# Moving work between TensorE, VectorE and the DMA queues in the last third of a long-convolution backward pass

## The chip, the cores and the metric

The kernel runs on one core of a Trainium2 chip. The metric is the device time of one execution in microseconds, the median of several runs. The profile that is read here is of one further execution.

## What is computed

The reference is a small network of two kinds of layer, run twice each, and its gradient. Layer A is a gated long convolution; layer B is a two-matrix MLP with SiLU. All tensors are bfloat16, sequence length 2048, width 448, hidden width 1792.

```python
def A(q, k, v, shift_k, ssm_k, ssm_D):
    k_shift = causal_conv(k, shift_k)            # 4 taps per channel
    kv = k_shift * v
    y = irfft(rfft(pad(kv)) * rfft(pad(ssm_k)))[:S]   # per channel, length 2*S
    return q * (y + kv * ssm_D)

def B(x, w1, w2):
    return silu(x @ w1) @ w2

x = A_q
x = x + A(layernorm(x), ...);  x = x + B(layernorm(x), ...)
x = x + A(layernorm(x), ...);  x = x + B(layernorm(x), ...)
# outputs: x, and the gradients of A_q, A_k, A_v, A_shift_k, A_ssm_k, A_ssm_D, B_w1, B_w2
```

The convolution does not depend on x, so its spectrum is computed once, and its gradient is computed once, from the summed gradient of y.

## The kernel before

There are three parts, one after the other in the code, which overlap on the chip.

The **prefix** (`_ssm_prefix`) makes the transforms of the filter and of kv on TensorE in two stages (16 points, then 128) and stores both spectra to HBM: `spec_K` and `spec_KV`, each 128 rows (64 real parts, 64 imaginary parts) of 14 chunks of 1024 columns. The product is transformed back into `Ysb`, which is y.

The **main part** (`Main.run`) goes over four chunks of 512 rows and does both layers forward and backward in each, in a woven order that is written out by hand. It stores the activations and their gradients to HBM for the weight gradients. A job generator (`Jobs.steps`) makes the weight gradients in steps of four matmuls of 128x448 (`ps_d`, L906); every step is called by hand between other TensorE work (`jobs.run(n)`). A block of 128 hidden units is eight steps, four with the operand of the second layer pair and four with that of the first. It needs two loads of 512 KB (`dstat`, L900), which SyncE's queue issues. The other operand stays in SBUF: `go` and `X` for the gradient of w2, `n3` and `n1` for that of w1. Blocks 0 to 6 of w2 come first, then the 14 blocks of w1, then blocks 7 to 13 of w2 (L948 to L963).

The **suffix** (`_ssm_suffix`, from L1050) makes the gradients of the convolution. In order:

- Stage 1 (L1068): 16 steps of two matmuls from `Ysb`, which by now holds the gradient of y, with a job step after each. Then `n3` is loaded (L1072, L979).
- Transposes (L1092): seven groups of 16, copied to Z by ScalarE and VectorE in turn, with a job step after each. The first three Z tiles are one tile, `Zw`.
- The inverse loop (L1133): seven rounds. Each round does the second transform stage of the next two chunks (`spectrum`, L1105) and then four products (`inverse`, L1118): for each of two chunks, the conjugate product with the KV spectrum and with the K spectrum. A product is two VectorE multiplications (`pa` with Z, `pb` with `xsw`, which is Z with real and imaginary halves exchanged) and 16 matmuls that accumulate both with two constant matrices (L226, L227). Three job steps follow each product. The spectra come in by `spec_load`, once a round, into two buffers.
- The deferred layer-norm rows (`APart`, L1015): the gradient of A_q needs eight row pairs, each with three loads and 16 VectorE operations. One pair goes behind the third group of transposes, one behind each round.
- gkv (L1163): the gradient of k_shift and of v. gK (L1181): the gradient of ssm_k, four pieces; of each, VectorE copies one column into `gKD`, which is stored as the gradient of ssm_D in elements of 2 bytes.
- The shift-kernel product (L1202): 224 matmuls with 32 columns each, then a reduction on VectorE (L1208 to L1219).
- The row loop (L1221): 16 groups on VectorE, which give the gradient of A_k.
- All job steps that are left (L1230).

TensorE executes in the order of the code (`manual_schedule`). On the other engines and the queues a planner orders the instructions, and `issue_after` ties one instruction behind another; each engine and each queue then works in that order. Large tiles share slots by tag in the pool `wk`: slot WY holds Ysb, then `n3`, then `go2` (the gradient operand for the last w2 blocks); slot WT holds `w2T`, then `Zw`, then `ksf`. A tile can only be written when the earlier one in its slot has been read for the last time.

Of the kernel before, what the change touches and what calls it, by code (L numbers as in the profile page):

```python
# [17 lines left out]
P = 128  # L18
S = 2048
D = 448  # L20
# [13 lines left out]
def make_fft_consts():  # L34
# [35 lines left out]
    def inv_pair(conj):  # L70
        sa = [1.0, 1.0] if conj else [1.0, -1.0]
        sb = [-1.0, 1.0] if conj else [1.0, 1.0]
        ga = build(lambda ci, co: sa[ci] * (Ct if co == 0 else St))
        gb = build(lambda ci, co: sb[ci] * (-St if co == 0 else Ct))
        return ga, gb

    GiA, GiB = inv_pair(False)
    GiAc, GiBc = inv_pair(True)
    GiBc = np.roll(GiBc, 64, axis=0)
    Gs = np.stack([G, GiA, GiB, GiAc, GiBc], axis=1)  # L80
# [3 lines left out]
G_FWD, G_IA, G_IB, G_IAC, G_IBC = range(5)  # L84
# [36 lines left out]
def kernel(  # L121
# [34 lines left out]
    k.SPEC_d = {nm: dram.tile([128, SPEC], BF16, name=f"spec_{nm}") for nm in ("K", "KV")}  # L156
# [15 lines left out]
    k.Gsb = keep.tile([P, 5, P], BF16, name="Gsb")  # L172
# [29 lines left out]
def _fft_stage1(k, n2, rhs, A1, psum, m=None):  # L202
    nc = k.nc
    ps = psum.tile([P, 2, 512], FP32, name="ps_s1", **k.pt["s1"])
    for c in range(2):
        nc.tensor.matmul(ps[:, c, :D], lhsT=k.M1sb[:, n2 if m is None else m, c, :], rhs=rhs, start=True, stop=True)
    _copy(nc, k.bal.pick(2 * D) if m is None else nc.scalar, A1[:, :, :, n2, :].rearrange("p dh c ds -> p c dh ds"), ps[:, :, :D].rearrange("p c (dh ds) -> p c dh ds", ds=4))

# [12 lines left out]
def _fft_inv_stage2_chunk(k, pa, pb, conj, B1, ci, psum, cnd=False):  # L221
    nc = k.nc
    ga, gb = (G_IAC, G_IBC) if conj else (G_IA, G_IB)
    pv = psum.tile([P, 8, P], FP32, name="ps_v", **k.pt["v"])
    for i in range(8):
        nc.tensor.matmul(pv[:, i, :], lhsT=pa[:, i * P:(i + 1) * P], rhs=k.Gsb[:, ga, :], start=True, stop=False)  # L226
        nc.tensor.matmul(pv[:, i, :], lhsT=pb[:, i * P:(i + 1) * P], rhs=k.Gsb[:, gb, :], start=False, stop=True)  # L227
    if cnd:
        _copy(nc, k.bal.pick(1024), B1[:, :, 32 * ci:32 * ci + 32].rearrange("p q (dh ds) -> p dh q ds", ds=4),
              pv[:].rearrange("p dh (q ds) -> p dh q ds", ds=4))  # L230
    else:
        _copy(nc, k.bal.pick(1024), B1[:, 8 * ci:8 * ci + 8, :].rearrange("p a b -> p (a b)"), pv[:].rearrange("p a b -> p (a b)"))


def _swap_halves(k, dst, src):
    k.nc.vector.tensor_copy(dst[0:64], src[64:128])
    return k.nc.vector.tensor_copy(dst[64:128], src[0:64])
# [41 lines left out]
def _ssm_prefix(k):  # L279
# [4 lines left out]
    with ExitStack() as es:  # L284
# [108 lines left out]
        def cons_ka(ci, ps):  # L393
            sl = slice(ci * 1024, (ci + 1) * 1024)
            _copy(nc, bal.pick(1024), Ka[:, sl], ps[:])
            if ci % 2 == 1:
# [3 lines left out]
                nc.gpsimd.dma_start(out=k.SPEC_d["K"][:, lo:hi], in_=Ka[:, lo:hi])  # L400
# [37 lines left out]
        def cons_prod(ci, ps):  # L438
# [3 lines left out]
            if ci % 2 == 1:  # L442
                st = nc.gpsimd.dma_start(out=k.SPEC_d["KV"][:, (ci - 1) * 1024:(ci + 1) * 1024], in_=Zf[:, (ci - 1) * 1024:(ci + 1) * 1024])
# [9 lines left out]
            if len(hold) > 2:  # L453
                pa, pb, cj = hold.pop(0)
                _fft_inv_stage2_chunk(k, pa, pb, False, B1, cj, psum)

        _fft_stage2(k, Zkv, psum, cons_prod)
        for pa, pb, cj in hold:
            _fft_inv_stage2_chunk(k, pa, pb, False, B1, cj, psum)
# [379 lines left out]
class Jobs:  # L839
# [78 lines left out]
    def group(self, fts, keys, movs, fin, tags=None):  # L918
        ps = {}
        tags = tags or [None] * len(fts)  # L920
        for i, ft in enumerate(fts):
            st = self.load(keys[0], ft)
            ps[ft] = self.bank(tags[i])
# [41 lines left out]
    def go2(self):  # L965
        k = self.k
        if not hasattr(self, "go2t"):
            self.go2t = k.wk.tile([P, NT, D], BF16, name="go2", tag="WY")
# [10 lines left out]
    def load_n3(self):  # L979
        k = self.k  # L980
        self.n3 = k.wk.tile([P, NT, D], BF16, name="n3m", tag="WY")
        k.nc.sync.dma_start(out=self.n3[:], in_=_pm(k.N_d[3][:]))
# [32 lines left out]
class APart:  # L1015
# [6 lines left out]
    def fetch(self):  # L1022
# [3 lines left out]
        for nm, src, bufs in (("g", k.G1_d, 2), ("n", k.N_d[0], 1), ("y", k.Y_d, 1)):  # L1026
# [234 lines left out]
```

## Time and profile before

| What | us |
|---|---|
| runs: median (lowest to highest) | 773.59 (770.3 to 775.28) |
| profiled execution | 769.31 |
| its span | 767.5 |
| stage 1 | 526 to 546 |
| transposes | 547 to 558 |
| inverse loop, gkv follows | 563 to 674 |
| gkv, gK | 674 to 709 |
| rest | 709 to 767 |

How to read the profile: PE is TensorE, PEld its weight loads, DVE is VectorE, ACT is ScalarE, POOL is GpSimd, SP is SyncE. A row names the code line, the operation and the tiles; in square brackets stands how long the engine had been idle before it and what it waited for. "issue" is idle time for which the profile shows no cause. Waits are listed as total, number, longest. The landing time of a DMA counts from its issue.

### The profile page before, as it was taken

Reading aid. Unit: us, or ns where it says so; the run is one execution under the profiler, and the core shown is the slowest. Engines: PE = TensorE matmul, PEld = TensorE weight load, DVE = VectorE, ACT = ScalarE, POOL = GpSimd, SP = SyncE. Lnnn points to the kernel's source line nnn. Section 1 sums busy time; section 2 is a strip of 40 time slices with the busy share of each in tenths; the row PEclk is TensorE's granted clock in tenths of the full one; section 3 lists DMA queues with packets and bytes.
Section 4 is the critical chain, followed back from the end, with each engine's and each line's share of the span. In section 5 each row is a group of like instructions: output and inputs, shape, how many; then the busy total and the mean of one; then the engine's idle time right before and its main releaser. Section 6 shows DMA issues by size and latency. Waiting matters only on the chain.

```text
span 767.5 us, 12748 instructions
## 1 busy us (share of the span) xinstructions
PE 707.8 (92%) x4991; PEld 398.6 (52%) x5020; DVE 476.4 (62%) x1137; ACT 459.2 (60%) x581; POOL 127.0 (17%) x213
## 2 busy tenths in 40 slices
PE   6998779999999999999999999999979999999594
PEld 4976534445444455444445445444646666656352
DVE  4789832857685758855487526444357767760497
ACT  5878767787957878587786772214645454454000
POOL 1144210210020100201001000001212322143211
PEclk9999989999999999999999999999989999999797
DMA  9959769479968996678975993498977897689861
GB/s 319 267 168 292 282 231 233 114 190 226 218 150 187 272 223 169 131 194 210 216 190 115 218 308 131 104 246 251 397 290 243 315 326 243 203 341 364 80 207 60
DMA packets 188653, 171.28 MB, mean 223 GB/s; under 512 B 135954, under 2 KB 166802, under 8 KB 187440
## 3 DMA queue, kind: packets, MB, share of 16 engines
q1 hardware_dynamic: 173984, 113.95, 56.9%
q0 software_dynamic: 14144, 56.50, 22.1%
q8 instruction: 39, 0.64, 0.3%
q14 instruction: 22, 0.18, 0.1%
q10 hardware_dynamic: 464, 0.00, 0.0%
HBM read 73.52 MB, written 60.10 MB: 174 GB/s over the span
## 4 chain that ended last, share of the span: by engine, by line
PE 62%; ACT 12%; DVE 9%; DMA 8%; issue 7%; POOL 2%; SPq 0%; POOLq 0%; ACTq 0%; DVEq 0%
PE ps_d L906 12%; PE ps_h L603 10%; PE ps_n L671 10%; PE ps_g L644 9%; PE ps_o L625 6%; ACT dT L618 3%; DMA n3m<-N_d 2%; PE ps_d L941 2%; DMA M1sb<-c_m 2%; PE ps_v L227 2%; PE ps_v L226 2%; PE ps_t L517 2%; ACT aT L606 1%; DVE ln_st L259 1%; ACT dT L111 1%
## 5 line engine op out<-in xcount | busy, mean ns | idle before, releaser
L906 PEld LDWEIGHTS <-dstat 128*128 128x128 bf16 x800 | 77.0, 99 | 72.4 <-issue 10.4
L603 PE MATMUL ps_h<-nT,w1sb 112*128 112x512 bf16 x448 | 104.4, 379 | 5.5 <-ACT dT L111 2.5
L644 PE MATMUL ps_g<-nT,w2T 128*128 128x512 bf16 x432 | 100.4, 381 | 1.3 <-ACT nT L518 0.2
L671 PE MATMUL ps_n<-w1T,ghT 128*128 128x448 bf16 x448 | 95.3, 353 | 1.8 <-DVE ghT L656 1.7
L625 PE MATMUL ps_o<-w2sb,aT 128*128 128x448 bf16 x448 | 88.8, 352 | 0.0
L654 ACT CAST ghT<-ps_g 128x1024 bf16<-128x1024 f32 (+1 forms) x68 | 54.5, 824 | 49.7 <-PE ps_g L644 49.7
L606 ACT ACTIVATE aT<-ps_h 128x1024 bf16<-128x1024 f32 (+1 forms) x72 | 58.4, 834 | 31.6 <-PE ps_h L603 30.8
L603 PEld LDWEIGHTS <-w1sb 112*128 112x128 bf16 x448 | 43.8, 98 | 58.3 <-issue 8.7
L644 PEld LDWEIGHTS <-w2T 128*128 128x128 bf16 x448 | 43.7, 99 | 50.9 <-issue 1.8
L831 DVE SCALAR_TENSOR_TENSOR lb_v<-lb_u,n 128x448 bf16<-128x448 bf16 x48 | 29.9, 624 | 64.1 <-ACT lb_u L675 63.6
L671 PEld LDWEIGHTS <-ghT 128*128 128x128 bf16 x448 | 43.2, 98 | 44.3 <-DVE ghT L656 4.0
L625 PEld LDWEIGHTS <-aT 128*128 128x128 bf16 x448 | 43.4, 98 | 39.8
L906 PE MATMUL ps_d<-n3m,dstat 128*128 128x448 bf16 x224 | 50.1, 362 | 5.4 <-DMA n3m<-N_d 5.0
L618 ACT ACTIVATE dT<-dT 128x1024 bf16<-128x1024 bf16 (+1 forms) x64 | 54.6, 936 | 0.1
L266 POOL TENSOR_TENSOR rstd<-ln_ve,mhalf 128x2 f32<-128x2 f32 (+2 forms) x27 | 22.6, 836 | 182.4 <-DVE ln_ve L264 182.4
L111 ACT CAST dT<-ps_h 128x1024 bf16<-128x1024 f32 (+1 forms) x59 | 52.1, 901 | 0.0
L906 PE MATMUL ps_d<-n1m,dstat 128*128 128x448 bf16 x224 | 47.8, 352 | 0.1
L226 PE MATMUL ps_v<-Gsb,pa 128*128 128x128 bf16 x336 | 42.9, 219 | 3.1 <-DVE pa L449 3.0
L227 PE MATMUL ps_v<-Gsb,pb 128*128 128x128 bf16 x336 | 42.2, 219 | 2.2 <-DVE pb L450 1.9
L518 ACT COPY nT<-ps_t 128x1024 bf16<-128x1024 bf16 (+1 forms) x28 | 28.3, 1012 | 20.8 <-PE ps_t L517 20.1
L675 ACT ACTIVATE lb_u<-ps_n,rstd 128x448 bf16<-128x448 f32 x32 | 20.7, 646 | 32.2 <-PE ps_n L671 18.1
L906 PE MATMUL ps_d<-X,dstat 128*128 128x448 bf16 x176 | 38.9, 363 | 0.0
(202 smaller groups left out, 1191.7 us busy)
## 6 DMA issues: line engine op xcount, KB each, us to landing
dstat<-g_d SPq DMA_DIRECT2D x28, 512.0 KB, 5.0
dstat<-a_d SPq DMA_DIRECT2D x26, 512.0 KB, 5.6
a_d<-turned SPq DMA_DIRECT2D x16, 512.0 KB, 3.8
g_d<-turned SPq DMA_DIRECT2D x16, 512.0 KB, 3.4
a_d<-turned SPq DMA_DIRECT2D x16, 384.0 KB, 3.1
g_d<-turned SPq DMA_DIRECT2D x16, 384.0 KB, 2.7
N_d<-n POOLq DMA_DIRECT2D x10, 448.0 KB, 5.0
spec_K<-Z POOLq DMA_DIRECT2D x7, 512.0 KB, 7.2
```

What stands on the lines that cost most here:

```text
L111: nc.scalar.copy(out, in_)
L226: nc.tensor.matmul(pv[:, i, :], lhsT=pa[:, i * P:(i + 1) * P], rhs=k.Gsb[:, ga, :], start=True, stop=False)
L227: nc.tensor.matmul(pv[:, i, :], lhsT=pb[:, i * P:(i + 1) * P], rhs=k.Gsb[:, gb, :], start=False, stop=True)
L603: nc.tensor.matmul(ps[:, u, :], lhsT=self.w1sb[:, dc, ft * P:(ft + 1) * P], rhs=nT[:DC, dc, :], start=(dc == 0), stop=(dc == ND - 1))
L606: self.last_silu = nc.scalar.activation(aT[hh][:, o:o + hi - lo, :], ps[:, lo:hi, :], ACT.Silu)
L618: self.nc.scalar.activation(d[:, o:o + n, :], d[:, o:o + n, :], ACT.Derivative_silu)
L625: nc.tensor.matmul(po[:, :D], lhsT=aT[ft // 7][:, ft % 7, tl * P:(tl + 1) * P], rhs=self.w2sb[:, ft, :], start=(ft == 0), stop=(ft == NF - 1))
L644: nc.tensor.matmul(ps[:, u, :], lhsT=self.w2T[:, b, ft * P:(ft + 1) * P], rhs=gT[:, b, :], start=(b == 0), stop=(b == ND - 1))
L654: nc.scalar.copy(g, ps[:, lo:hi, :])
L671: nc.tensor.matmul(pn[:, :D], lhsT=gh[ft // 7][:, ft % 7, tl * P:(tl + 1) * P], rhs=self.w1T[:, ft, :], start=(ft == 0), stop=(ft == NF - 1))
L831: nc.vector.scalar_tensor_tensor(out=v[:], in0=u0, scalar=-1.0 / D, in1=n_t, op0=ALU.mult, op1=ALU.mult, accum_out=cp[:, 1:2])
L906: self.nc.tensor.matmul(ps[:, :D], lhsT=st[:, t, :], rhs=mov[:, t, :], start=(first and t == 0), stop=(last and t == NT - 1))
```

## The change

**Inverse.** The spectrum store becomes one tensor of 128 rows x 14 chunks x (K, KV) x 1024. `spec_load` is called for each chunk in place of each pair: it makes two transfers to 128 partitions, the 64 real rows written to both halves, and the 64 imaginary rows written to both halves. The two buffers keep their size, so each holds one chunk. VectorE forms the whole complex product: `q = Z * real`, `q2 = xsw * imaginary`, `q = q + q2`; the exchange of halves now also negates one half. TensorE does eight matmuls a product, with one constant matrix. There are four buffers for q and q2 together, where pa and pb had five. The copies out of PSUM are given to ScalarE by name.

**Operands.** `n3` and `go2` move to slot WT, `Zw` and `ksf` to slot WY. `n3` is loaded when block 5 of w2 begins, in the queue behind that block's first load.

**Rows.** `APart` is set up before stage 1; row pairs are also run behind steps 6 and 11 of stage 1, and `q_g` has three buffers.

**Tail.** The gKD copies go from VectorE to ScalarE. Three job steps follow each of the four parts of the shift-kernel product. Its reduction and its two stores move into the row loop, behind group 11.

```diff
-    k.SPEC_d = {nm: dram.tile([128, SPEC], BF16, name=f"spec_{nm}") for nm in ("K", "KV")}
+    k.SPEC_d = dram.tile([128, NCI, 2, 1024], BF16, name="spec")
...
+    GiQ = build(lambda ci, co: (Ct, -St)[ci] if co == 0 else (St, Ct)[ci])
...
 def _swap_halves(k, dst, src):
     k.nc.vector.tensor_copy(dst[0:64], src[64:128])
-    return k.nc.vector.tensor_copy(dst[64:128], src[0:64])
+    return k.nc.vector.tensor_scalar(out=dst[64:128], in0=src[0:64], scalar1=-1.0, scalar2=None, op0=ALU.mult)
...
         for i, ft in enumerate(fts):
             st = self.load(keys[0], ft)
+            if fts == (5, 6) and i == 0:
+                self.load_n3()
...
-            self.go2t = k.wk.tile([P, NT, D], BF16, name="go2", tag="WY")
+            self.go2t = k.wk.tile([P, NT, D], BF16, name="go2", tag="WT")
...
-        self.n3 = k.wk.tile([P, NT, D], BF16, name="n3m", tag="WY")
-        k.nc.sync.dma_start(out=self.n3[:], in_=_pm(k.N_d[3][:]))
+        self.n3 = k.wk.tile([P, NT, D], BF16, name="n3m", tag="WT")
+        with k.tc.issue_after(self.last_ld.ins):
+            k.nc.sync.dma_start(out=self.n3[:], in_=_pm(k.N_d[3][:]))
...
-        for nm, src, bufs in (("g", k.G1_d, 2), ("n", k.N_d[0], 1), ("y", k.Y_d, 1)):
+        for nm, src, bufs in (("g", k.G1_d, 3), ("n", k.N_d[0], 1), ("y", k.Y_d, 1)):
...
+        ap = APart(k, e1.enter_context(tc.tile_pool(name="qp", bufs=1, reuse_waits="tile")))
         for n2 in range(16):
             k.M1sb = k.m1h[n2 // 8]
-            _fft_stage1(k, n2, gY[:, n2, :], A1, psum, n2 % 8)
+            mm1 = _fft_stage1(k, n2, gY[:, n2, :], A1, psum, n2 % 8)
             jobs.run(1)
-        jobs.load_n3()
+            if n2 in (6, 11):
+                ap.run(1, mm1)
...
-            def spec_load(cp):
-                lo, hi = cp * 2048, (cp + 1) * 2048
-                nc.gpsimd.dma_start(out=kk[:, 0, :], in_=k.SPEC_d["K"][:, lo:hi])
-                nc.gpsimd.dma_start(out=kk[:, 1, :], in_=k.SPEC_d["KV"][:, lo:hi])
+            def spec_load(ci):
+                for c in range(2):
+                    src = k.SPEC_d[64 * c:64 * c + 64, ci].rearrange("(o p) m n -> o p (m n)", o=1).to_broadcast([2, 64, 2048])
+                    nc.gpsimd.dma_start(out=kk[:, c].rearrange("p m n -> p (m n)"), in_=src)
...
-                    for spec_t, B1, cnd in ((t[1], B1k, True), (t[0], B1v_, False)):
-                        pa = p1.tile([P, 1024], BF16, name="pa", tag="pab", bufs=5)
-                        pb = p1.tile([P, 1024], BF16, name="pb", tag="pab", bufs=5)
-                        nc.vector.tensor_tensor(out=pa[:], in0=Zf[cp][:, o], in1=spec_t[:, o], op=ALU.mult)
-                        last = nc.vector.tensor_tensor(out=pb[:], in0=t[2][:, o], in1=spec_t[:, o], op=ALU.mult)
-                        bal.add("dve", 2.2)
-                        _fft_inv_stage2_chunk(k, pa, pb, True, B1, ci, psum, cnd=cnd)
+                    for m in (1, 0):
+                        q = p1.tile([P, 1024], BF16, name="q", tag="pab", bufs=4)
+                        q2 = p1.tile([P, 1024], BF16, name="q2", tag="pab", bufs=4)
+                        nc.vector.tensor_tensor(out=q[:], in0=Zf[cp][:, o], in1=kks[ci][:, 0, m, :], op=ALU.mult)
+                        nc.vector.tensor_tensor(out=q2[:], in0=xsw[:, o], in1=kks[ci][:, 1, m, :], op=ALU.mult)
+                        last = nc.vector.tensor_tensor(out=q[:], in0=q[:], in1=q2[:], op=ALU.add)
+                        pv = psum.tile([P, 8, P], FP32, name="ps_v", **mm)
+                        for i in range(8):
+                            nc.tensor.matmul(pv[:, i, :], lhsT=q[:, i * P:(i + 1) * P], rhs=k.Gsb[:, G_IQ, :], start=True, stop=True)
...
                         jobs.run(3)
+                    if ci + 2 < NCI:
+                        kks.append(spec_load(ci + 2))
...
-            nc.vector.tensor_copy(gKD[:, dc:dc + 1], gK[:, 0:1])
+            nc.scalar.copy(gKD[:, dc:dc + 1], gK[:, 0:1])
...
                     nc.tensor.matmul(pd[32 * b:32 * b + 32, 0, P * r0:P * r0 + P], lhsT=gks[:, sl_, ch], rhs=kx[:, sl_:sl_ + 4, ch], start=(sl_ == 0), stop=(sl_ == 15))
-        junk = p2.tile([P, 4, 4, 32], FP32, name="skjunk", tag="gka")
-        jobs.run(4)
+            jobs.run(3)
...
+            if g != 11:
+                continue
+            junk = s_[:].rearrange("p a d -> p (a d)")[:, 0:512].rearrange("p (r u c) -> p r u c", u=4, c=32)
...
```

## The prediction

> **What bounds the kernel now.** I read the busy totals first, then TensorE's waits in the last third of the span (only code there changes much), then the busy time by stage, then VectorE in order of time, then the landing times of the spectra.
>
> ```profile
> PE 707.8 (92%) x4991; PEld 398.6 (52%) x5020; DVE 476.4 (62%) x1137; ACT 459.2 (60%) x581; POOL 127.0 (17%) x213
> ```
>
> TensorE is the bound on average; the question is which of its work and waits from 526 us on go away. Its waits between 520 and 770 us:
>
> ```profile
> PE ps_sk L1207 <- issue: 7.7, 1, 7.7
> PE ps_d L906 <- DMA n3m<-N_d: 5.0, 1, 5.0
> PE ps_gkv L1169 <- ACT gkv L1171: 1.8, 1, 1.8
> PE ps_sk L1207 <- DVE gKD L1193: 0.7, 1, 0.7
> ```
>
> Four single waits, 15.2 us. The stages (columns: stretch, length, busy us of PE, PEld, DVE, ACT, POOL, granted clock, DMA share, GB/s):
>
> ```profile
> 546.00:563.00 17.00, 11.92 (x142) 8.95 (x140) 9.47 (x20) 7.38 (x7) 2.71 (x5) 0.96 1.01 417
> 563.00:575.00 12.00, 11.61 (x65) 6.00 (x66) 6.49 (x10) 5.36 (x6) 0.54 (x1) 0.77 0.66 242
> 591.36:606.84 15.48, 15.43 (x132) 9.96 (x132) 10.98 (x28) 7.92 (x11) 5.23 (x9) 1.00 0.78 259
> 606.84:622.31 15.47, 15.42 (x132) 9.96 (x132) 10.97 (x27) 7.91 (x11) 3.58 (x7) 1.00 0.97 370
> 709.00:720.00 11.00, 3.42 (x212) 3.27 (x212) 0.05 (x1) 1.70 (x3) 2.55 (x4) 0.79 1.06 101
> 740.00:767.00 27.00, 17.41 (x93) 8.81 (x90) 23.35 (x27) 1.60 (x3) 4.88 (x9) 0.86 0.23 80
> ```
>
> The reader is to see that one round of the inverse loop (15.48 us, seven rounds) is all TensorE, with VectorE at 10.98; that both long waits lower the granted clock after them; and that at the end VectorE, not TensorE, is the busy one. Why, in VectorE's timeline:
>
> ```profile
> 708.89 0.16 DVE L1193 COPY gKD<-gK 112x1 bf16<-112x1 bf16 x1 [8.24 <-ACT gK L111]
> 721.05 0.75 DVE L1212 TENSOR_TENSOR skjunk<-ps_sk,skmask 128x384 f32<-128x384 f32 x2 [12.00 <-PE ps_sk L1207]
> 763.07 0.63 DVE L1226 TENSOR_TENSOR B1v<-gka 128x448 bf16<-128x448 f32 x1
> ```
>
> From 691 to 721 it stands behind four tiny copies and the shift-kernel product, then runs the row loop (L1223 to L1226, 2.66 us a row) to 763.7. TensorE's last result is copied at 757.49 and issued at 758.33; VectorE's last store is issued at 763.99.
>
> **Part by part**, against the profiled execution: 769.31 us, span 767.5. It lies 4.28 under the median of the runs, 773.59, so the final sum is scaled by 773.59/769.31.
>
> *n3 into the slot of w2T.* Before, its load issues at 546.23, when stage 1 has read Ysb, and lands 16.9 us later. The new slot was last read near 514, and SP issues the load behind that of block 5 at 529.10. Even 16.9 us later it is there at 546; it is needed at 558. Gone: 5.0 us, and the slow clock behind it: rounds of 2.30, 2.34 and 1.54 us (563.17 to 569.35) where a warm one takes 1.19, so 2.6. Together -7.6. Queued behind n3 on SP are three a loads and g loads (512 KB each); the first is needed at 540.4, and 2.9 MB at 319 GB/s take 9.1 us from 529.1, so it fits by 2 us. Zw, which changes places with n3, must now wait for stage 1's last read at 546.2; its first copy is at 548.30, so that costs nothing, and ksf and go2 follow the same tiles as before. What is late next: the first product's chain, a copy of 1.01, two swaps of 1.39, a product and a sum of 0.69 each, against some 2.4 us of TensorE work: +1.5 (0 to 3).
>
> *Deferred-norm rows earlier.* Two of eight row pairs move into stage 1, where VectorE is idle for 18.5 us before its copy at 548.30; each is 4.73 us of work. Their q loads land in 6.7 to 8.5 us there and have one buffer for n and y, so the second pair waits for the first, and the pair behind group 2 for the second. VectorE runs in order: if the second pair sits ahead of the Z copies, TensorE's transposes wait. Bounds 0 and 8 (one q landing, 8.5); I take +2.5, nearer zero because the 18.5 idle us hold both pairs' 9.5. On POOL the first pair's three loads (1.6 us of issue) go ahead of Minvs, not needed before 674, and of kk, needed at 560. In return rounds 6 and 7 carry no rows. The third buffer of q_g takes away POOL's six waits for the out store (29.1 us together), which lie on no path.
>
> *Single product.* A product's 16 matmuls take 0.89 us here, between job blocks:
>
> ```profile
> 571.30 0.22 PE L226 MATMUL ps_v<-Gsb,pa 128*128 128x128 bf16 x1
> 572.19 2.43 PE L906 MATMUL ps_d<-n1m,dstat 128*128 128x448 bf16 x12
> ```
>
> Eight of the 16 go: 28 x 0.445 = -12.45, and a round becomes 15.48 - 1.78 = 13.7. ACT's copies stay (all 28 are on ACT now). VectorE gains four sums a round at 0.606 spacing (2.42), and each sum needs the product before it, 0.115 later than a free one (0.45): 13.85. The swap's second half becomes a multiply by -1; no row shows that one. Its bounds are the copy (0.69 for 64x2048) and twice that, since the tensor_scalar of 128x448 (L834, 0.395) costs as much as a tensor_tensor of the same shape (0.391). I take the copy's end for the likeliest, since both run one input from SBUF, and keep 0.54 a round for the range: 13.85 to 14.4 with rows, 9.1 to 9.7 without. So VectorE passes TensorE by 0.15 to 0.7 in the five rounds with rows: 0.8 to 3.5.
>
> [...]
>
> *Spectra.* Bytes double: 28 loads of 512 KB for 14, on the same two buffers, each for one chunk, not two. POOL issues two more a round (0.54 each, it is busy under 5.3 of 15.5). A buffer's cycle is landing, 0.54 for the second issue, and four products with sums, 3.9 us; it must fit 13.7, so a load may take 9.3 us. The present ones:
>
> ```profile
> DMA to landing us min/median/max: 3.6/7.6/11.0
> DMA to landing us min/median/max: 3.9/6.6/18.0
> ```
>
> The medians (kk_c, then kk_d) fit; the loads beside ksf (9.9 and 11.0, at 370 GB/s) miss by up to 1.7; the 18.0 fell in the stretch at 417 GB/s. A round now moves 1.8 MB of dstat, 2.1 of spectra, 0.9 of rows, 0.2 of results, 5.05 MB: 369 GB/s at 13.7 us. The trace has held 417 for 17 us, so it can be moved, with little to spare. For VectorE and the buffers together I give back +4 of the 12.45 (0 to 12.45).
>
> [...]
>
> *gkv.* The 1.8 wait is for gks, whose load POOL issues at 676.28 behind the last rows' store (it waited 6.80 for it). The rows end two rounds sooner: -1.75 (0 at worst).
>
> *Shift-kernel product.* 212 small matmuls run in 3.42 us, then 7.7 us "issue". The DMA view from 709 to 713 has two instruction transfers and from 713 to 720 none; there queue 0 holds the engines for 113.6% with only 64 packets, while the gKD store (0.9 KB) needs 16.1 us and the gK store 15.0. I read it as TensorE running out of instructions while stores block the queues. After the change 12 job steps lie between its four blocks, so a block's 64 pairs and 12 job pairs, 152 instructions, go in 3.3 us: 46 per us in place of 124. The store itself stays. Gone: 7.7, 0.74, and the slow clock after it (20 matmuls from 720.94 in 6.04 us where 3.79 is warm: 2.25), -10.7; I leave +1.5 (0 to 10.7).
>
> *End.* gKD goes to ACT (four copies of about 0.2, hidden in its idle time) and the reduction (2.1 us, and two POOL issues of 0.81 and 0.55, which now go ahead of the last two row stores and delay none that is ready) behind row 11, so VectorE's 16 x 2.66 + 2.1 = 44.7 us begin when gkv ends; TensorE has 69.8 - 10.7 = 59 from there. VectorE is hidden by 14 us, and waits 2 for the product. TensorE's results end: the last issue is 5.66 earlier, its landing 4.0 where 2.2: -3.9. Were that cover gone, the end would be VectorE's again, 3.9 later.
>
> *Prefix.* Spectra stores in runs of 2 KB, not 4: VectorE already waits 2.7 for one (L557): +0.5 (0 to 3).
>
> **Sum**: -7.6 +1.5 +2.5 -12.45 +4 -1.75 -10.7 +1.5 -3.9 +0.5 = -26.4; 742.9 on the profiled scale, x 773.59/769.31 = 747.0.
>
> **Rivals.**
> 1. The loop gains nothing: VectorE with 13.85 to 14.4 and the buffers hold it at 15.48. For it: three resources within 5%. Against: TensorE needs a product only every 2.7 us and two lie ready. 742.9 + 8.45 = 751.4, 755.5 scaled.
> 2. The pause in the shift-kernel product survives, since the store that I blame stays: 742.9 + 9.2 = 752.1, 756.3 scaled.
> 3. Slower: the spectra's landing sets the round. At landing L it is L + 4.44. It eats the whole gain at 13.7 + 0.57 + 26.4/7 = 18.0, so from L = 13.6. For it: 13.7 and 18.0 are in the trace, at DMA saturation, and demand is 369 GB/s. Against: two of fourteen loads. At L = 16 a round is 20.4, 7 x 6.7 - 4 = 43 us more: 786, 790 scaled.
> 4. Nothing is given back: 732.9, 737 scaled.
>
> **How the numbers follow.** Forecast 0.45, rival 1 0.2, rival 2 0.15, rival 4 0.1, rival 3 0.1. The range runs from rival 4's 737 to 765, which takes in rivals 1 and 2, each alone and both together (764.8); outside lie rival 3 and a part of rival 4. Within 1% (about what a measurement of this kernel can tell from no change) means 765.9 to 781.3: only a mild form of rival 3 or all give-backs together. Faster 0.86, same 0.06, slower 0.08.
>
> **What would show it.** No wait of ps_d for n3m, and clock 1.00 at 563; 224 matmuls fewer, rounds of 13.7 to 14.5 us; waits of ps_v for the sums or of VectorE for kk in their place if rival 1 or 3 holds; no pause inside ps_sk; last in the chain a dout store. It would be wrong if TensorE waits at ps_tr for Z copies behind rows, or if kk lands later than 10 us throughout.

## The result, and the profile after

The changed kernel takes 890.49 us (median of 4 runs, 889.39 to 891.3), the kernel before 774.34 us on the same chip (4 runs, 770.3 to 775.28): a ratio of 1.1503, 95% interval 1.1459 to 1.1548. Forecast were 747.0 us, in a range of 737 to 765. It is 143.5 us slower than forecast, and on the other side of the kernel before.

The profiled execution after has a span of 889.0 us and a mean granted clock of 0.917 (767.5 us and 0.979 before). Start with what TensorE waited for, over the whole span. Columns: waiting instruction <- what ended the wait: us in total, times, longest.

```profile
PE ps_v L1125 <- DVE q L1122: 89.1, 9, 14.9
PE ps_tr L1091 <- DVE Zw L1095: 23.8, 1, 23.8
PE ps_d L896 <- issue: 6.9, 2, 6.5
PE ps_tr L1091 <- DVE Zg L1095: 5.7, 1, 5.7
```

The wait for n3 is gone, as forecast. In its place stand 89 us in the products, for VectorE's sums, and 30 us in the transposes, for VectorE's copies of Z. VectorE is not full there; it waits too, for loads:

```profile
DVE q_y L1035 <- DMA q_y<-Y_d: 96.2, 7, 27.4
DVE q L1120 <- DMA kk_c<-spec: 41.6, 3, 14.8
```

So look at the loads. From the page: two of its DMA counts (packets and MB), and two lines of its list of DMA issues, with the median us from issue to landing last:

```profile
DMA packets 215755, 178.65 MB, mean 201 GB/s; under 512 B 161266, under 2 KB 192114, under 8 KB 214544
...
q0 software_dynamic: 41248, 63.91, 24.3%
...
kk_c<-spec POOLq DMA_DIRECT2D x14, 512.0 KB, 19.7
kk_d<-spec POOLq DMA_DIRECT2D x14, 512.0 KB, 19.0
```

The loads have the size of those before (512 KB), and land in 19 to 20 us instead of 7.6 and 6.6. The rows' loads, whose shape the change leaves alone, are late with them: the median landing of q_y is 19.1 us, before it was 4.7. Yet the engines are not full. The stretches of the loop, with engine busy time, TensorE's granted clock (PEclk), the share of the 16 DMA engines that is busy, and GB/s:

```profile
600.00:640.00 40.00, 25.70 (x156) 13.73 (x155) 22.89 (x45) 13.40 (x15) 9.12 (x14) 0.81 0.55 146
640.00:680.00 40.00, 25.14 (x161) 14.14 (x160) 14.98 (x33) 12.26 (x16) 6.96 (x10) 0.79 0.74 180
680.00:720.00 40.00, 17.30 (x91) 9.36 (x90) 15.96 (x38) 7.10 (x9) 9.14 (x13) 0.66 0.62 169
```

146 to 180 GB/s, where the loop before moved 261 on the mean (563 to 674), and a DMA share of 0.55 to 0.74: the loads are slow although the engines have time left. The packet counts point at a reason. Before, queue 0 sent 14144 packets for 56.50 MB; now it sends 41248 for 63.91. Packets under 512 B are 25312 more (161266 - 135954), some 900 for each of the 28 spectra loads. In the trace they have 4 bytes: queue 0 has 28098 packets of that size, 2786 before. What brings them is shown below (x2).

The early row work stands in VectorE's timeline (start, duration, operation, and in brackets the idle time before it and what ended it):

```profile
543.25 0.69 DVE L1035 SCALAR_TENSOR_TENSOR q_y<-q_g,rstd,q_y 128x448 bf16<-128x448 bf16 x1 [12.39 <-DMA q_y<-Y_d]
...
575.86 0.69 DVE L1035 SCALAR_TENSOR_TENSOR q_y<-q_g,rstd,q_y 128x448 bf16<-128x448 bf16 x1 [27.41 <-DMA q_y<-Y_d]
...
580.99 1.22 DVE L1095 COPY Zw<-ps_tr 128x2048 bf16<-128x2048 bf16 x1
```

The second pair's q_y load is issued at 548.46, between the first two spectra loads (535.73 and 551.78), and lands only at 575.86. VectorE makes its first copy of Z behind that pair: at 580.99 instead of 548.30.

In the tail the four blocks of the shift-kernel product now run without a gap, but the pause follows right behind them (TensorE's timeline):

```profile
845.54 1.07 PE L1208 MATMUL ps_sk<-kx_s,gks 128*32 128x128 bf16 x32
846.54 0.55 PE L896 MATMUL ps_d<-X,dstat 128*128 128x448 bf16 x2
847.44 0.35 PE L896 MATMUL ps_d<-X,dstat 128*128 128x448 bf16 x1 [0.35 <-issue]
854.33 4.26 PE L896 MATMUL ps_d<-X,dstat 128*128 128x448 bf16 x13 [6.54 <-issue]
```

And one line settles a doubt of the forecast, the swap's second half: 0.69 us, the rate of a copy.

```profile
604.74 0.69 DVE L227 TENSOR_SCALAR xsw_c<-Zw 64x2048 bf16<-64x2048 bf16 x1
```

### The profile page after: what moved, and what is told of

It reads as the page before. It is cut to its first block, busy times and chain, and to the rows that moved or that the text cites. A ratio compares the mean times of both kernels' runs of the same rounds, so it can differ in the third digit from the quotient of the medians.

```text
span 889.0 us, 12374 instructions
## 1 busy us (share of the span) xinstructions
PE 718.9 (81%) x4796; PEld 394.3 (44%) x4796; DVE 494.2 (56%) x1161; ACT 459.6 (52%) x585; POOL 145.4 (16%) x227
## 2 busy tenths in 40 slices
DMA packets 215755, 178.65 MB, mean 201 GB/s; under 512 B 161266, under 2 KB 192114, under 8 KB 214544
## 3 DMA queue, kind: packets, MB, share of 16 engines
q0 software_dynamic: 41248, 63.91, 24.3%
## 4 chain that ended last, share of the span: by engine, by line
PE 42%; DMA 22%; issue 12%; DVE 11%; ACT 9%; POOL 3%; POOLq 0%; SPq 0%; DVEq 0%; ACTq 0%
DMA kk_c<-spec 9%; PE ps_h L593 9%; PE ps_n L661 8%; PE ps_g L634 8%; PE ps_o L615 6%; DMA q_y<-Y_d 4%; DMA out_dram<-q_g 3%; PE ps_d L896 3%; ACT dT L608 2%; DMA kk_d<-spec 2%; PE ps_d L933 2%; PE ps_t L507 1%; ACT aT L596 1%; DMA turned<-ghT 1%; DMA q_n<-N_d 1%
## 5 line engine op out<-in xcount | busy, mean ns | idle before, releaser
L896 PEld LDWEIGHTS <-dstat 128*128 128x128 bf16 x800 | 80.8, 104 | 87.5 <-issue 26.3
L634 PE MATMUL ps_g<-nT,w2T 128*128 128x512 bf16 x448 | 103.1, 384 | 0.7 <-ACT nT L508 0.7
L1125 PE MATMUL ps_v<-Gsb,q 128*128 128x128 bf16 x224 | 20.4, 244 | 89.1 <-DVE q L1122 89.1
L1035 DVE SCALAR_TENSOR_TENSOR q_y<-q_g,rstd,q_y 128x448 bf16<-128x448 bf16 x16 | 10.3, 683 | 96.2 <-DMA q_y<-Y_d 96.2
L1125 PEld LDWEIGHTS <-q 128*128 128x128 bf16 x224 | 16.7, 110 | 97.0 <-DVE q L1122 93.2
L896 PE MATMUL ps_d<-n1m,dstat 128*128 128x448 bf16 x224 | 54.6, 389 | 0.0
L896 PE MATMUL ps_d<-n3m,dstat 128*128 128x448 bf16 x224 | 54.1, 384 | 0.0
L1127 ACT CAST A1g<-ps_v 128x1024 bf16<-128x1024 f32 x14 | 14.2, 1012 | 70.3 <-PE ps_v L1125 70.3
L896 PE MATMUL ps_d<-X,dstat 128*128 128x448 bf16 x176 | 40.7, 372 | 6.9 <-issue 6.9
## 6 DMA issues: line engine op xcount, KB each, us to landing
kk_c<-spec POOLq DMA_DIRECT2D x14, 512.0 KB, 19.7
```

The lines of the kernel that those rows point to most:

```text
L634: nc.tensor.matmul(ps[:, u, :], lhsT=self.w2T[:, b, ft * P:(ft + 1) * P], rhs=gT[:, b, :], start=(b == 0), stop=(b == ND - 1))
L896: self.nc.tensor.matmul(ps[:, :D], lhsT=st[:, t, :], rhs=mov[:, t, :], start=(first and t == 0), stop=(last and t == NT - 1))
L1125: nc.tensor.matmul(pv[:, i, :], lhsT=q[:, i * P:(i + 1) * P], rhs=k.Gsb[:, G_IQ, :], start=True, stop=True)
```

## The experiments

The theory, a supposition that nothing above shows: `to_broadcast([2, 64, 2048])` makes a source whose outermost dimension is 2, and such a load runs on only 2 of the 16 DMA engines (F). Rivals: the doubled bytes (B), and the order, by which the early rows hold VectorE whatever the loads do (O).

**x1_two_halves**: the same bytes, as loads of 64 plain rows.

```diff
-  src = k.SPEC_d[64*c:64*c+64, ci].rearrange(...).to_broadcast([2, 64, 2048])
-  nc.gpsimd.dma_start(out=kk[:, c]..., in_=src)
+  for o in range(2):
+      nc.gpsimd.dma_start(out=kk[64*o:64*o+64, c], in_=k.SPEC_d[64*c:64*c+64, ci])
```

> The changed kernel with each transfer to 128 partitions cut into two transfers to 64 (same bytes, same rows read twice, 56 issues in place of 28). Theory F (few engines: a source that repeats 64 rows is carried by 2 of the 16 DMA engines, and all that POOL issues later waits behind it): the spectra land in 4 to 10 us in place of 15 to 24, and the time falls to the prediction's 740 to 765. Rival B (bytes: twice the spectra are too much for the DMA engines beside the other loads): landings stay over 13 us, the time over 860. Rival O (order: the early rows block VectorE whatever the loads do): landings fall, but the wait of ps_tr for Z copies stays near 24 us, 775 to 800.

Measured: 790.4 us (788.55 to 793.88), ratio to the kernel before 1.0226 (1.019 to 1.0262). 100.1 of the 116 us are gone, with twice the number of loads and the same bytes. Packets of queue 0, the landings of kk_c and kk_d, and TensorE's waits in the transposes:

```profile
q0 software_dynamic: 16608, 63.81, 26.3%
DMA to landing us min/median/max: 3.6/7.8/16.3
DMA to landing us min/median/max: 7.4/9.3/12.8
PE ps_tr L1091 <- DVE Zw L1095: 6.5, 1, 6.5
PE ps_tr L1091 <- DVE Zg L1095: 4.0, 1, 4.0
```

The time misses F's 740 to 765 and lies in O's range, but O's sign is not there: the waits of ps_tr for Z copies fall from 29.5 to 10.5 us. The landings are F's in the median. Packets under 512 B are 136627, 673 more than before for 42 more loads: about 16 for each additional load.

**x2_before_twice64**: the other way round, the kernel before with its 14 loads made of 64 rows sent twice (the second half of the rows is not loaded).

```diff
-  nc.gpsimd.dma_start(out=kk[:, 0, :], in_=k.SPEC_d["K"][:, lo:hi])        # and KV
+  nc.gpsimd.dma_start(out=kk[:, i, :], in_=k.SPEC_d[nm][0:64, lo:hi].rearrange("(o p) n -> o p n", o=1).to_broadcast([2, 64, 2048]))
```

> The kernel before, with the source of each of its 14 spectra loads replaced by 64 rows repeated twice (the second half of the rows is left out of the computation; count, bytes and destinations as before). Theory F: landings of 13 to 24 us and some 900 four-byte packets per load more; the time rises, by less than in the changed kernel since a buffer has a whole round: 790 to 850. Rival B: bytes are as before, so landings stay at 4 to 11 us and the time within 1% of before.

Measured: 838.78 us, ratio 1.087 (1.08 to 1.0939), median landings of 21.8 (kk_c) and 18.5 us (kk_d) at the bytes and the number of loads of the kernel before. The page:

```profile
q0 software_dynamic: 26688, 56.55, 21.4%
```

26688 - 14144 = 12544, which is 896 for each of the 14 loads, and for 0.05 MB more (56.55, before 56.50) some 4 bytes each. 896 is 14 x 64: what F would give if each of 14 engines without data had one packet for each of the 64 rows. The count of the changed kernel comes out in the same way: 28 x 896, and 16 for each of the 14 additional loads (as in x1), are its 25312. The trace does not name a packet's engine, so that two engines carry the rows is read into these counts, not shown. B is out as the main cause.

**x3_shapes**: the same in the kernel before, with the outermost dimension 16, 16, 16, 8, 4, 2 and 2 in the seven rounds (one execution, 814.66 us; the rows that are not loaded are left out).

> The kernel before with a different repeat for the loads of each round: 16 times 8 rows (first three rounds' loads), 8 times 16, 4 times 32, 2 times 64 (the last two); the other rows are left out of the computation, bytes are the same. Theory F, with as many engines as there are repeats: landings of about 4 to 8 us at 16 repeats, 5 to 9 at 8, 8 to 12 at 4, 13 to 20 at 2. Rival B: no order by repeats. A third way: any repeated source is slow alike, 13 to 20 us in all.

Landings, first and second load of a round, us: 16 (third round) 5.3 and 7.0; 8: 11.3 and 10.0; 4: 23.0 and 26.2; 2: 18.8 and 19.3, 18.2 and 19.7. (The second round's, also 16, took 17.3 and 24.4; they are issued at 541 to 544, into the stretch in which the kernel before had its 18.0.) With 16 a load is as quick as a plain one (medians of 7.6 and 6.6 in the kernel before), with 8 slower, with 4 and 2 about three times as slow. For 8 and 4 that is more than F's 5 to 9 and 8 to 12. The loads with 4 can't be compared with the others: POOL issues them right behind the load of ksf (1792 KB, 617.04, 12.4 us to landing), and how much of their 23.0 and 26.2 us is theirs stays open. The count fits F: if n repeats use n engines and each of the other 16 - n gets 128/n small packets, the loads with 8, 4 and 2 give 2 x 8 x 16 + 2 x 12 x 32 + 4 x 14 x 64 = 4608, and the page has 18752 - 14144 = 4608. So the counts agree with F in sum for repeats of 16, 8, 4 and 2; no run here has another, and the number of engines itself stays a reading. That rows are read more than once is not the cause: x1 reads its rows twice too (medians of 7.8 and 9.3 us to landing), and 16 repeats of 8 rows landed in 5.3 and 7.0.

**x4_no_early_rows**: x1 without the two row pairs in stage 1.

```diff
-            if n2 in (6, 11):
-                ap.run(1, mm1)
```

> As x1_two_halves, but the two row pairs behind steps 6 and 11 of stage 1 go back to the rounds of the loop. Theory F: within 10 us of x1, no wait of ps_tr for Z copies over 3 us; if the early rows cost as I had put it (+2.5), x4 is faster by some 2 us or slower by what two more rounds with rows cost (0.5 to 3). Rival O: faster than x1 by 15 us or more.

Measured: 781.9 us, ratio 1.0096 (1.0061 to 1.0132); 8.5 less than x1, and no wait of ps_tr for Z copies is left. The early rows cost more than the forecast's 2.5, but O's 15 were not reached.

With plain loads, x4 still stood 35 us over the forecast. The next runs take the forecast's terms one by one.

**y1_slot**: the kernel before with the new place of n3's load alone.

```diff
-  self.go2t = ..., tag="WY");  self.n3 = ..., tag="WY");  Zw = ..., tag="WT");  ksf = ..., tag="WT")
+  self.go2t = ..., tag="WT");  self.n3 = ..., tag="WT");  Zw = ..., tag="WY");  ksf = ..., tag="WY")
-  jobs.load_n3()                                  # behind stage 1
+  if fts == (5, 6) and i == 0: self.load_n3()     # in group, behind block 5's load
```

> The kernel before with the changed place of n3's load alone: Zw and ksf in buffer WY, go2 and n3 in WT, n3's load issued in the group of blocks 5 and 6; loop, row work and tail are those of before. Theory that the forecast's other terms hold and only the loads failed: the wait of 7.6 us for n3 is gone and nothing takes its place, 765 to 768 us against 774. Rival: the wait is given back, for the following waits are set by VectorE and by landings and not by PE's order: 772 to 776 us. If slower than 777, the longer life of WT or WY makes another load late.

Measured: 770.58 us, ratio 0.998 (0.9942 to 1.0019). Of the expected 7.6 us at most 4.5 are there, perhaps none: it lies between theory and rival. Its trace is of an execution of 1375.83 us and is not used here.

**y2_tail**: the new tail alone.

```diff
-  nc.vector.tensor_copy(gKD[:, dc:dc + 1], gK[:, 0:1])
+  nc.scalar.copy(gKD[:, dc:dc + 1], gK[:, 0:1])
+      jobs.run(3)            # behind each of the four ps_sk blocks
-  junk = ...; jobs.run(4)    # the reduction, ahead of the row loop
+  if g == 11: junk = ...     # the reduction, inside the row loop
```

> The kernel before with the changed tail alone: the column copies of gKD on ScalarE, three steps of the planner behind each ps_sk block, and the reduction of ps_sk behind step 11 of VectorE's row loop. Theory that the forecast's terms hold: pause 10.7 less 1.5 left, end 3.9, gkv 1.75, together about 15 us: 758 to 762 us. Rival (the pause survives and only moves behind the blocks): 5.6 us at most, 767 to 772 us, with a ps_d or ps_sk matmul that waits over 5 us for nothing that the profile shows. Third: the row loop on VectorE or its stores end the kernel: 771 or more.

Measured: 763.96 us, ratio 0.9893 (0.9862 to 0.9924): -8.3 us, between the theory's 758 to 762 and the rival's 767 to 772. TensorE's wait in the product:

```profile
PE ps_sk L1207 <- issue: 10.3, 4, 5.2
```

The pause survives (7.7 before), as the rival had it. The gain is then the shorter end and what the steps between the blocks cover; the two were not taken apart.

**y3_row_store**: the kernel before, with gKD stored in rows.

```diff
-  nc.gpsimd.dma_start(out=k.outs[6].rearrange("(c p) -> p c", p=DC), in_=gKD[:])     # 448 elements of 2 bytes
+  nc.tensor.transpose(pt[:ND, 0, :DC], gKD[:], k.ident[:DC, :DC])
+  nc.scalar.copy(gDr[:], pt[:ND, 0, :DC])
+  nc.gpsimd.dma_start(out=k.outs[6].rearrange("(c p) -> c p", p=DC), in_=gDr[:])      # 4 rows of 224 bytes
```

> The kernel before with one edit: gKD (112 partitions x 4) is transposed on TensorE to 4 partitions x 112 and stored in 4 rows of 224 bytes, where before 448 elements of 2 bytes went out one by one. Theory: it is the store of single elements that stalls the DMA engines and starves PE of instructions, so the wait inside ps_sk (8.9 us, ended by issue) falls under 2 us and the time to 764 to 768 us. Rival: the wait comes with PE's instruction transfers or with the other stores at that place: it stays over 6 us, and the time within 3 us of 774.

Measured: 767.26 us, ratio 0.9938 (0.9909 to 0.9967): -4.8 us. The wait inside ps_sk of this run:

```profile
PE ps_sk L1210 <- issue: 2.8, 1, 2.8
```

And the stretch around it, first of this run, then of the kernel before (there with TensorE's busy time alone, then granted clock, DMA share, GB/s):

```profile
700.00:720.00 20.00, 15.00 (x331) 11.24 (x329) 0.31 (x2) 5.53 (x8) 6.37 (x11) 0.99 0.77 276
```

```profile
700.00:720.00 20.00, 11.74 (x293) 0.88 1.04 217
```

The small store was the main cause: its landing falls from 16.1 to 5.1 us, the pause from 7.7 (not the expectation's 8.9) to 2.8, and the DMA share from 1.04 to 0.77 while more is moved (276 GB/s, not 217). The expected 2 us were missed by 0.8. In the trace's packet records from 700 to 760 no packet of 4096 B on queue 0 takes over 0.9 us; with the 2-byte store in place some take 7.9 (before) and 6.0 (y2). The rows of y3 go out at 716, in the middle of the product (713.3 to 720.1), so it is not that the store has merely moved out of the way.

**y4_half_loads**: x4 with the loads of the second half left out and the second multiply reading the first half's tile.

```diff
-  for c in range(2):
+  for c in range(1):
-  nc.vector.tensor_tensor(out=q2[:], in0=xsw[:, o], in1=kks[ci][:, 1, m, :], op=ALU.mult)
+  nc.vector.tensor_tensor(out=q2[:], in0=xsw[:, o], in1=kks[ci][:, 0, m, :], op=ALU.mult)
```

> The run of x4 (changed kernel, each spectra load cut in two of 64 partitions, no early rows: 781.9 us) with the loads of the spectra's second half left out: the second multiply of each product reads the first half's tile, so g_k and g_v are not computed as in the reference; every instruction of VectorE, PE and ScalarE stays. Theory that what is left over (35 us over the forecast) is the doubled bytes of the loads: 745 to 755 us, and the waits of ps_v for VectorE fall from 25 us to under 8. Rival: it is VectorE's own chain (multiply, multiply, add ahead of each product): 777 to 784 us, with the waits of ps_v as they are. In between, both have a share.

Measured: 769.11 us, ratio 0.9959 (0.9924 to 0.9995): 12.8 less than x4 (10.6 by the ratios, see below); neither theory's number. The waits of ps_v for VectorE fall from 25.1 to 12.2 us. The edit halves the number of loads along with the bytes, and the two were not told apart.

**z2_no_sums**: y4 with the 28 sums left out.

```diff
-  last = nc.vector.tensor_tensor(out=q[:], in0=q[:], in1=q2[:], op=ALU.add)
```

> The run of y4 (changed kernel, half the spectra loads, no early rows: 769.1 us) with the 28 sums of the products left out: PE multiplies the first product's tile, so the spectral products are not the reference's; both multiplies and all matmuls stay. Theory that VectorE's longer chain (three operations ahead of each product, about 17 us of sums in all) takes back the matmuls that were saved: 750 to 758 us, ps_v's waits for VectorE under 4 us (12.2 in y4). Rival: the loop goes by landings and ScalarE's copies: 765 to 770 us.

Measured: 765.43 us, ratio 0.9903 (0.9866 to 0.9941). Only 3.7 less, as the rival had it: behind loads that come late, VectorE's sums do not eat the gain. (The sums were not left out where loads land in time, as in w1 below.) In their place VectorE waits 19.0 us for kk, 7.3 in y4:

```profile
DVE q L1118 <- DMA kk_c<-spec: 9.9, 5, 4.1
DVE q L1118 <- DMA kk_d<-spec: 9.1, 3, 6.4
```

A load is asked for when two chunks earlier is done, half a round ahead; the kernel before asks a whole round ahead.

**z3_slot_tail**: the kernel before with the edits of y1 and y2, loop as before.

> The kernel before with the new place of n3's load and the new tail, the loop as before: what the changed kernel is without its single product and its early rows. If y1 and y2 add: 760 to 763 us, no wait of PE for n3, about 10 us of waits for issue left in and behind ps_sk. Then the single product at half loads (y4, 769.1) costs 6 to 9 us instead of the 8.45 that the forecast took off. Rival: the slot is worth the forecast's 7.6 once the tail doesn't wait: 755 to 758 us.

Measured: 760.72 us, ratio 0.9873 (0.9806 to 0.9941). Slot and tail add up, as expected. No wait for n3; the pause stands behind the product (8.3 us, a ps_d matmul, ended by issue).

**z1_all**: the edits of y1, y2 and y3 together.

> The kernel before with the new place of n3's load (y1: -2 us), the new tail (y2: -9 us) and gKD stored in 4 rows (y3: -6 us), and with the loop's two products, its loads and its row work as before. If the three add, less what y2 and y3 take of the same pause (the wait for issue is 7.7 us before, 2.8 with the rows): 755 to 760 us against 773. Rival: the tail's gain is the pause alone, which both take: 761 to 765 us.

Measured: 753.31 us (750.22 to 756.95), ratio 0.9772 (0.9732 to 0.9813), under the expected 755 to 760. It is the quickest version found, 137 us under the change as made, and no wait of TensorE for issue is left in it at that place.

**w1_loads_of_before**: x4 with the spectra loaded as before, whole rounds ahead, and so with half the bytes of the change.

```diff
-  def spec_load(ci):   # four loads of 64 rows a chunk, issued two chunks ahead
+  def spec_load(cp):
+      for u in range(2):
+          nc.gpsimd.dma_start(out=kk[:, u], in_=k.SPEC_d[:, 2 * cp + u])
...
+  in1=kks[cp][:, u, m, :]          # in both multiplies
```

> The run of x4 (changed kernel without early rows) with the spectra loaded as in the kernel before: two plain loads of 128 partitions a round (512 KB each), a whole round ahead; both multiplies of a product read the same tile, so g_k and g_v are not computed as in the reference, but every instruction of VectorE, PE and ScalarE is that of the changed kernel's loop. It is the forecast's own condition (loads as before) with its early rows taken away. Theory that only the loads failed the forecast's loop: 747 to 754 us, the waits of ps_v for VectorE under 4 us in all (12.2 in y4, whose loads of the same bytes are issued half a round ahead), and the stretch from the last ps_tr to the first ps_gkv 96 to 100 us (116.3 before, 112.0 in y4). Rival: VectorE's sums take the gain back whatever the loads do: 758 to 766 us, ps_v's waits 8 us or more, the stretch 105 or more.

Measured: 760.96 us, ratio 0.9838 (0.9799 to 0.9877). Half of each: the loop is right as the theory had it (99.8 us, waits of ps_v 3.1), the time as the rival. TensorE's waits, and the end of the loop in the timeline:

```profile
PE ps_gkv L1166 <- ACT gkv L1168: 11.4, 1, 11.4
PE ps_sk L1204 <- issue: 8.5, 1, 8.5
PE ps_v L1121 <- DVE q L1118: 3.1, 3, 1.3
```

```profile
656.90 0.92 PE L1166 MATMUL ps_gkv<-B1v,Minvs 128*128 128x448 bf16 x4
...
660.93 0.39 DVE L826 TENSOR_TENSOR q_g<-lb_v,q_g 128x448 bf16<-128x448 bf16 x1
...
661.62 0.55 POOL L1040 DMA_DIRECT2D out_dram<-q_g  x1 [7.74 <-DMA dstat<-a_d]
...
664.49 1.07 POOL L1145 DMA_DIRECT2D gks<-in_A_v_dram  x2 [0.44 <-issue]
...
674.39 1.70 DVE L1171 TENSOR_TENSOR gks<-gkv,gks 128x896 bf16<-128x896 bf16 x3 [10.69 <-DMA gks<-in_A_v_dram]
```

TensorE is at gkv at 656.90, but the last row pair ends on VectorE at 661.3. Its store holds POOL's queue for 7.74 us (the releaser named, a load of SP's, is not the one: the store's source is written at 660.93). Behind the store stand the tail's loads; gks lands at 674.4. So 9 us of loop became 9.6 us more of wait.

**v1_early_rows** (w1 with the change's early rows: the forecast's condition, but for the doubled bytes) and **v2_pair_at_2** (w1 with two pairs behind the third round) ask whether that last pair is the cause.

```diff
+            if n2 in (6, 11):                                   # v1
+                ap.run(1, mm1)
-                ap.run(1, inverse(cp, prev))                    # v2
+                ap.run(2 if cp == 2 else 1, inverse(cp, prev))
```

> The run w1 (changed kernel, plain loads of half the bytes, both multiplies of a product reading the same tile, so g_k and g_v are not the reference's; 761.0 us) with the change's two early row pairs put back: the forecast's condition whole, 747.0 us by its sum. Theory that the last row pair in the last round holds the tail's loads: rounds 6 and 7 then carry no rows, the wait of ps_gkv (11.4 us) falls under 4, and what the early pairs cost at the transposes (8.5 us between x1 and x4, less here, for the queues are emptier) is 2 to 5 us: 752 to 757 us. Rival (the tail's loads are bound by their bytes, whoever issues them): ps_gkv still waits 8 us or more, and the early rows' cost comes on top: 762 to 767 us.

> The run w1 (761.0 us, both multiplies of a product reading the same tile) with two row pairs behind the third round instead of one, so that the last round carries none and no pair runs ahead of the transposes. Theory that the last row pair holds the tail's loads: the wait of ps_gkv falls from 11.4 us to under 5, and 753 to 757 us. Rival (bytes of the tail, or VectorE, which is busy 18 of 20 us in the third round, passes the loss on): ps_v's waits grow by 3 us or more, or ps_gkv still waits 8: 759 to 763 us.

Measured: v1 760.38 us, ratio 0.9878 (0.9835 to 0.9921); v2 761.28 us, ratio 0.9906 (0.9869 to 0.9943). TensorE's waits of v1, then of v2:

```profile
PE ps_tr L1089 <- DVE Zw L1093: 10.4, 1, 10.4
PE ps_sk L1206 <- issue: 4.2, 1, 4.2
PE ps_tr L1089 <- DVE Zg L1093: 2.6, 1, 2.6
```

```profile
PE ps_v L1121 <- DVE q L1118: 10.6, 6, 5.0
PE ps_sk L1204 <- issue: 8.3, 2, 4.8
```

In both the wait of ps_gkv is gone, so the last pair was its cause. And in both the time stays, for v1 between theory and rival: the loss moves to the transposes (v1) or to the products (v2), as v2's rival had it. In v2 VectorE is the full engine from 640 to 660, 18.94 us of 20 against TensorE's 16.16:

```profile
640.00:660.00 20.00, 16.16 (x111) 8.92 (x110) 18.94 (x48) 8.30 (x11) 3.09 (x5) 0.93 0.60 192
```

All runs side by side, from the tile view's first and last starts of ps_tr and ps_gkv (us of one profiled execution each; the time is the median). The runs were made on several chips, on which the kernel before took 769.7 to 774.3 us; where a difference of two times is small, the difference of their ratios to the kernel before on the same chip is the better one:

| kernel | transposes | last ps_tr to first ps_gkv | gkv | sum | time |
|---|---|---|---|---|---|
| before | 10.7 | 116.3 | 13.1 | 140.1 | 774.34 |
| changed | 44.1 | 202.8 | 11.2 | 258.1 | 890.49 |
| x1: 64 plain rows a load | 24.9 | 128.1 | 11.3 | 164.3 | 790.4 |
| x4: and no early rows | 10.8 | 130.1 | 16.8 | 157.7 | 781.9 |
| y4: and half the bytes | 10.8 | 112.0 | 18.3 | 141.1 | 769.11 |
| w1: and a round ahead | 10.8 | 99.8 | 24.8 | 135.4 | 760.96 |
| v1: w1 with early rows | 25.3 | 98.6 | 11.2 | 135.1 | 760.38 |
| v2: w1, pair moved | 10.8 | 110.9 | 11.2 | 132.9 | 761.28 |
| z3: loop of before, slot, tail | 10.8 | 108.8 | 13.1 | 132.7 | 760.72 |
| z1: and gKD in rows | 10.7 | 108.9 | 13.1 | 132.7 | 753.31 |

Read the sums: with loads of half the bytes, a round ahead, the changed loop, with or without early rows, needs 132.9 to 135.4 us for this stretch, and the loop of before needs 132.7. The single product makes the loop shorter, and the stretch no shorter.

## Why the prediction was wrong, point by point

**Spectra: the step that failed.** The forecast took the landings of the loads before (medians 7.6 and 6.6) for the new loads, since their size was the same, and saw the doubled bytes as the only danger. It did not look at the shape of the source. The landings were 19.7 and 19.0: rival 3's mechanism (landing sets the round, slower from 13.6 us on), though it came with the shape of the source (x1's plain loads land in 7.8 and 9.3) and at a DMA share of 0.55 to 0.74 (600 to 720), not at saturation. From the change to x1 this is 100.1 us. Rival 3's formula gives 19.4 + 4.44 = 23.8 us a round; measured were 202.8/7 = 29.0. The formula has no term for the rows' loads, which VectorE waited for too, 48.3 us in the loop; the rest was not taken apart further. The last sentence of the forecast, kk later than 10 us throughout and transposes that wait for Z copies behind rows, named both signs.

**VectorE and the buffers, +4: too little.** With plain loads, the doubled bytes and the half round's lead cost 30.0 us more (x1 790.4 to v1 760.4; 26.9 by the ratios); without early rows the bytes are 12.8 (x4 to y4; 10.6) and the lead 8.2 (y4 to w1; 9.4), each with a smaller number of loads in it. In the stretch of x1's loop from 600 to 700 the DMA view gives a share of 0.9 or more in 36 of 40 slices at 268 GB/s: the forecast's argument from 417 GB/s, seen at the transposes, did not hold for this mix of transfers.

**Early rows, +2.5 (0 to 8): too little.** 8.5 in x1; in v1 14.5 us at the transposes (25.3 against 10.8), of which the freed gkv gives back 13.6. It rested on q loads of 6.7 to 8.5 us; VectorE waited 12.0 for one in v1.

**Single product, -12.45: right in the loop, lost behind it.** 108.8 us with two products (z3), 99.8 with one (w1): -9.0, about what -12.45 + 4 said. But the rows then end late, and gkv, forecast at -1.75, waits 11.4. The forecast asked what is late next for n3, but not for VectorE's rows and POOL's queue. In effect this is rival 1, at another place.

**Shift-kernel product, -10.7 + 1.5: wrong.** Rival 2 was right: 6.9 us of pause in the changed kernel, 10.3 in y2, 8.3 + 1.3 in z3. Spreading the instructions did not shorten the pause; the store that the forecast itself blamed had to go (y3, z1). That TensorE runs out of instructions meanwhile is still a reading: the trace gives no cause for "issue".

**n3, -7.6.** The wait is gone in the changed kernel and in z3, whose stretch is 7.4 us shorter than before (132.7 to 140.1). In the time of y1 alone only -1.5 (-4.5 to +1.5) can be seen; where the rest goes there stays open.

**End, -3.9.** The order is as forecast: in the changed kernel VectorE's row loop is through at 867 and TensorE's last blocks at 883. The -3.9 was not measured alone; together with what the blocks cover the tail gives -8.3 (y2). **The swap** is at a copy's rate (0.69 us, as the copy of the other half): the 0.54 us a round that the range kept for it was not needed. The prefix's +0.5 was not tried.

By sums: 890.5 measured; less 100.1 for the shape of the loads (98.9 by the ratios), less 30.0 (26.9) for bytes, number and lead of the loads, is v1's 760.4. That is 13.4 us over the forecast, 17.9 by the ratio. In v1's trace the early rows are 12.0 over the forecast (14.5 at the transposes), the pause 4.5 (6.0 us of issue waits, where 1.5 was left), and the loop is 3.2 under it (98.6, where 116.3 - 7.6 + 1.5 - 12.45 + 4 gives 101.8). That makes 13.3; the rest is not taken apart. So even with the loads that it had in mind, at half the bytes, the forecast ends near rivals 1 and 2 together (764.8 by its text), inside the range.

## What to carry to other kernels

A DMA's size does not give its time: look at its shape too, above all where a source is repeated (in x2 loads of the same 512 KB landed in 18.5 and 21.8 us, not 6.6 and 7.6), and count packets (there 896 more of some 4 bytes for each load went with it). Before a saving on the bounding engine is booked, follow who else must be done for the next stage to begin, here the rows on VectorE, their store on POOL, and the loads queued behind it. Where a pause is put down to a transfer, try the transfer itself: here storing 448 elements as 4 rows took 4.9 us off the pause, reordering the matmuls around it took off none (10.3 us in y2).

## What the runs showed of the hardware that was not expected

- A load of 512 KB whose source has an outermost dimension of 2 brings 896 more packets of some 4 bytes (12544 more on queue 0 for 14 loads, with 0.05 MB). Its median landing is 18.5 and 21.8 us instead of 6.6 and 7.6 (x2).
- One store of 448 elements of 2 bytes (0.9 KB) needs 16.1 us to land. Beside it other packets, of 4096 B, take as much as 7.9 us (their median on queue 0 is 0.16), and TensorE stands for 7.7 us; as 4 rows of 224 B it lands in 5.1, no such packet takes over 0.9, and TensorE stands for 2.8.
- With twice the bytes in 64-row loads the engines were over 90% busy at 268 GB/s, where the kernel before had held 417 for 17 us at the transposes (x1, 600 to 700; before, 546 to 563).
